# A routed expert layer behind linear attention: the fullest expert's left rows join its own job, and rows are asked for one job further ahead

## The chip, the cores and the metric

The kernel runs on one core of one Trainium2 chip. The time is the device time of one launch in microseconds (us), the median of a few runs. A separate, profiled execution gives the trace that is read below; its own time stands beside its span, the stretch from the first instruction to the last.

A core has five engines that run their own instruction streams and meet at semaphores: PE (matrix products), DVE and ACT (element-wise work on 128 partitions), POOL (element-wise work, and DMAs whose addresses come from an index list) and SP (here a queue that issues DMAs). In the profile "PEld" is PE's weight load.

## What is computed

Linear attention, normalised, followed by a layer of eight experts in which each row goes to one expert. Cut to what matters:

```python
# q, k, v: (8, 8, 576, 64)
kv  = einsum('bhsd,bhse->bhde', k, v)
out = einsum('bhsd,bhde->bhse', q, kv)
out = out / sqrt(mean(out * out, -1) + 1e-6) * g_norm
x = out.transpose(0, 2, 1, 3).reshape(4608, 512)

logits = x @ w_gate                      # 4608 x 8
expert = argmax(logits, 1)
gate   = softmax(logits)[row, expert]
for e in range(8):                       # w1[e]: 512 x 1024, w2[e]: 1024 x 512
    rows = expert == e
    y[rows] = gate[rows] * (relu(x[rows] @ w1[e]) @ w2[e])
```

How many rows an expert gets depends on the data. The inputs are drawn with a fixed seed.

## The kernel before

**Attention, 36 slots.** The 4608 rows are taken in 36 slots of 128 rows, nine to a pair of batches. k, v and q of one batch are each one load of 1.18 MB through SP (`load`, L201, issued at L207) into ten landing buffers `land`. For each batch PE forms k-transposed times v (`kv_mm`, L235, 64x64 tiles, L244). For each slot POOL brings q into order (`x_qp`, L297, instruction L302), PE transposes it (`x_qt`, L308, L312), ACT copies it, PE multiplies it with kv (`x_mm`, L326, L335). ACT and DVE normalise. The order of the slots and of all work inside them is written out by hand (`plan`, the lists `mid`, `late`, `last`, L810 to L894): POOL orders q three slots ahead, the transposition runs two slots ahead, and the kv products of a batch are spread over the four slots from the sixth before its first slot.

**Routing.** `Route` (L388) finds each row's expert and its rank among that expert's rows, and POOL scatters each row (1032 bytes: 512 half-precision values, the row's number, the sum for its gate) to place `expert * 4608 + rank` of a table `xs` in HBM (`scatter`, L480, L483). Places that get no row must not hold stray numbers. `blank_rows` (L221) therefore writes, early in the attention stage, 128 empty rows ahead of row 608 of each expert from a constant `c_zero` (L222), and the marks of the 32 rows that follow (L228). Both DMAs stand in SP's queue between the loads of k and v of batch 3 and that of q of batch 3 (L930 to L932).

**Expert jobs.** The experts are worked off one after the other, each as one job (`Job`, L634) of at most 608 rows (`CAP`), whatever the data: `CT` = 5 blocks of 128, 128, 128, 128 and 96 rows. The expert with the most rows among the last four (`FIXED` = 4) changes places with expert 7 and comes last; which it is, a chain of small DVE operations finds once all rows are counted (`left_over_table`, L526). SP reads the expert's number from it into a register (`expert_at`, L776).

A job consists of:
- `fetch` (L644): a transposing DMA of the job's rows from `xs` into `xt` (L654), and a small DMA of the rows' numbers and sums, `mt` (L662). `xt` has three buffers.
- `one` (L707): the first product. For each of two column ranges of 304 rows and eight blocks of the hidden size, four matmuls (L698) into `hp` (four buffers) and a relu on ACT (L710) into `ht`, a part of `xh`.
- `two` (L738): the second product. For each block of rows, eight matmuls of 512 columns (L743) into `yp` (four buffers), a DVE multiplication with the gate into `ys` (L748), and a scatter of the rows to the output on POOL (L751).
- `place` (L674): three small DVE operations that turn `mt` into indices and gates.

The weights of each expert are two loads of 2 MB (L159 for w1, L165 for w2) through SP into five staging buffers, taken in a fixed order by `load_next` (L191). While job n runs its products, DVE casts w1 of job n+1 (L171) and ACT casts its w2 (L182).

Job 0 is woven into the end of the attention stage (L985 to L1038). The order of the rest is the loop at L1044: at its head `jobs[n + 2].fetch()`, then the first product, a weight load, the second product, for n = 0 the table, then `place` of the next job and another weight load. So in SP's queue the rows of job n+2 stand behind the weight loads that job n-1 issued.

**The left rows.** Rows of the last expert beyond 608 form a job of their own, `left_over(32, ...)` (L782), of up to 128 rows. It runs seventh, just ahead of the last expert, with that expert's weights: POOL gathers the rows (L625), PE transposes them (L770) inside job 6, and both products follow on their own. Should rows still be left, a loop on a register (L1085) takes them 128 at a time.

Of the kernel before, what the change touches and what calls it, by code (L numbers as in the profile page):

```python
# [28 lines left out]
def kernel(  # L29
# [20 lines left out]
    CAP = 608  # L50
    EARLY = 384
    NE = EARLY // 128
    NOV = (N - CAP) // 128 + 1
    WIDTHS = [128, 128, 128, 128, 96]
# [14 lines left out]
    c32 = np.zeros((128, 128 + 8 + 8 + CT + 36 + 1 + 32), np.float32)  # L69
# [15 lines left out]
    c32[:, o_t:o_t + 32] = np.arange(32)  # L85
    c_f32 = nc.inline_tensor(c32, name="c_f32")
# [10 lines left out]
    zr = np.zeros((32, 4, RW // 2), np.float32)  # L97
    zr[:, :, RW // 2 - 1] = 1.0
    c_zero = nc.inline_tensor(zr.reshape(32, 2 * RW).view(np.int32), name="c_zero")
# [15 lines left out]
    tcol = cf[:, o_t:o_t + 32]  # L115
    ident16 = ch[:, 0:128]
# [10 lines left out]
    nvf = fixed("nvf", [128, 33], F32)  # L127
# [3 lines left out]
    tabb = fixed("tabb", [128, 33], F32)  # L131
    tabi = fixed("tabi", [128, 2, 40], I32)
    blank = fixed("blank", [128, RW // 2], I32)
    xo_bufs = [fixed(f"xo{n}", [128, RW], F16) for n in range(2)]
# [10 lines left out]
    xh = [fixed(f"xh{n}", [128, 8 * CAP], F16) for n in range(2)]  # L145
# [3 lines left out]
    order = list(range(E - 1)) + ["left", E - 1]  # L149
# [36 lines left out]
    W = [Weights(e, n) for n, e in enumerate(range(E))]  # L186
    W.append(W[E - 1])
# [33 lines left out]
    def blank_rows():  # L221
        nc.sync.dma_start(  # L222
            xs.ap().rearrange("(e s) c -> e s c", e=E)[:, CAP - 128:CAP, :].rearrange(
                "e (p r) c -> e p (r c)", r=4
            ),
            _bc(c_zero.ap(), 0, E),
        )
        nc.sync.dma_start(  # L228
            xs.ap().rearrange("(e s) c -> s e c", e=E)[CAP:CAP + 32, :, 256:258],
            _bc(blank[0:32, 256:258], 1, E),  # L230
        )
# [294 lines left out]
    def left_over_table():  # L526
# [16 lines left out]
        def pick(out, what):  # L543
# [28 lines left out]
        )  # L572
        nc.vector.tensor_scalar(
            nvf[:, 32:33], most_n, -float(CAP), None, op0=ALU.add
        )
        nc.vector.tensor_scalar(
            tabb[:, 32:33], who, float(N), float(CAP), op0=ALU.mult, op1=ALU.add
        )
        nxt = PW.tile([128, 8], F32, tag="nxt")
        nc.vector.tensor_scalar(nxt, most, 128.0, float(CAP), op0=ALU.mult, op1=ALU.add)  # L580
# [16 lines left out]
        cmb = PW.tile([128, 32, 8], F32, tag="cmb")  # L597
# [12 lines left out]
        nc.vector.reduce_sum(nvf[:, 0:32], cm, axis=AXX)  # L610
        nc.vector.scalar_tensor_tensor(
            out=nvf[:, 0:32], in0=tk, scalar=-128.0, in1=nvf[:, 0:32], op0=ALU.mult, op1=ALU.add
        )
        nc.vector.tensor_scalar(tabi[:, 0, 8:40], te, 7.0, None, op0=ALU.min)
        sb = tabb[:, 0:32]
# [18 lines left out]
    class Job:  # L634


        def __init__(self, nt, w, n, row, okm, bgm, views):
            self.nt, self.w, self.row = nt, w, row
            self.n = n
            self.okm, self.bgm, self.views = okm, bgm, views  # L640
            self.cols = CAP if nt > 1 else 128
            self.spans = [(0, 304), (304, CAP)] if nt > 1 else [(0, 128)]

        def fetch(self, t0=0, t1=None):  # L644
            nt = self.nt
            t1 = nt if t1 is None else t1
            if t0 == 0:
                self.xt = PW.tile([128, 4, CAP], F16, tag="xt", bufs=3, name="xt")
                self.mt = PW.tile([128, nt, 2], I32, tag=f"mt{nt}", bufs=4, name="mt")
            c0, c1 = 128 * t0, min(128 * t1, CAP)  # L650
# [17 lines left out]

            for go in (marks, rows) if self.n > 1 else (rows, marks):
                did = go()  # L670
                if t1 == NE:
                    early_reads.append(did)

        def place(self, t0=0, t1=None, okm=None, bgm=None):  # L674
# [11 lines left out]
            )  # L686
            nc.vector.tensor_tensor(self.idx[:, t0:t1], self.raw[:, t0:t1], bgm, op=ALU.add)
# [50 lines left out]
        def two(self, t, yp=None):  # L738
            m = WIDTHS[t]
            if yp is None:  # L740
                yp = PSF.tile([128, D], F32, tag="yp", bufs=4, name="yp")
            for f in range(8):
# [3 lines left out]
                )  # L746
            ys = PW.tile([128, D], F32, tag="ys", bufs=5, name="ys")
# [380 lines left out]
```

## Time and profile before

| | |
|---|---|
| median of 3 runs | 271.66 us (271.3 to 273.56) |
| profiled execution | 271.03 us, span 269.1 us |
| PE busy | 242.2 us (90%), 2708 matmuls |
| ACT busy | 155.2 us (58%) |
| DVE busy | 143.9 us (53%) |
| POOL busy | 107.5 us (40%) |
| granted clock of PE | 0.999 |
| moved by DMA | 82.93 MB, mean 308 GB/s |
| weight loads, 2 MB each | 16, median 12.6 us from issue to landing |
| transposing loads of rows | 9, median 9.7 us from issue to landing |

How to read it: a line of the timeline gives start (us), length (us), engine, line of the kernel, operation, what is written and what is read, and how many instructions were merged; in brackets the idle time of the engine before it and what ended it. "SPq" is a DMA issue in SP's queue: its length is the time that SP is held by it, not the transfer. "Landing" is the time from the start of an issue to the semaphore that tells of its end.

The page's rows of slices, 6.7 us each (busy tenths of PE and of DMA):

```profile
PE   5996799899999987689699999999899999999992
DMA  7999999999999999496799999999999999942023
```

The attention stage fills slices 1 to 20, the expert jobs those behind them.

### The profile page before, as it was taken

The numbers are of one execution on the slowest core, as the hardware profiler recorded it, in microseconds if no ns is written. First come the engines' busy times: TensorE is split into PE (matmuls) and PEld (weight loads), VectorE is DVE, ScalarE is ACT, GpSimd is POOL, SyncE is SP. The second block draws the span as 40 slices with busy tenths as digits, with TensorE's granted clock in tenths as the row PEclk, the third lists the DMA queues.
The fourth block names the chain that finished last, engine by engine and source line by source line (L and its number), as shares of the span: only waits on it lengthen the run. The fifth ranks groups of instructions, "written<-read, shape, count | busy, mean of one in ns | idle before, by whom it ended". The sixth has DMA issues, their size and how long they took to land. (4 is left out here: it accounts for less than half of the span.)

```text
span 269.1 us, 6877 instructions
## 1 busy us (share of the span) xinstructions
PE 242.2 (90%) x2708; PEld 170.4 (63%) x2708; DVE 143.9 (53%) x374; ACT 155.2 (58%) x359; POOL 107.5 (40%) x138
## 2 busy tenths in 40 slices
PE   5996799899999987689699999999899999999992
PEld 1575688788878876554457466574564756747740
DVE  1004277688787769988728991453604525343031
ACT  1053668567677748688248648287284692754800
POOL 8032222387378286557511060522404415042142
PEclk9999999999999999999999999999999999999999
DMA  7999999999999999496799999999999999942023
GB/s 241 333 391 391 392 426 369 394 397 392 393 382 407 415 384 355 161 274 256 168 221 410 250 328 417 277 384 332 362 420 277 375 314 322 285 125 104 14 79 110
DMA packets 52002, 82.93 MB, mean 308 GB/s; under 512 B 27739, under 2 KB 27995, under 8 KB 51944
## 3 DMA queue, kind: packets, MB, share of 16 engines
q1 hardware_dynamic: 46464, 67.95, 75.9%
q0 software_dynamic: 5056, 14.26, 14.3%
q8 instruction: 22, 0.36, 0.6%
q10 hardware_dynamic: 448, 0.26, 0.5%
q14 instruction: 12, 0.10, 0.1%
HBM read 63.37 MB, written 16.04 MB: 295 GB/s over the span
## 5 line engine op out<-in xcount | busy, mean ns | idle before, releaser
L751 POOL DMA_INDIRECT out_dram<-ys,idx x41 | 41.2, 1005 | 95.3 <-DVE ys L748 86.1
L710 ACT ACTIVATE xh<-hp 128x304 f16<-128x304 f32 (+1 forms) x120 | 49.2, 413 | 46.3 <-PE hp L698 33.2
L743 PE MATMUL yp<-w2b,xh 128*128 128x512 f16 (+1 forms) x304 | 67.1, 379 | 0.6 <-ACT xh L734 0.6
L698 PEld LDWEIGHTS <-w1b 128*128 128x128 f16 x544 | 51.7, 98 | 22.6 <-issue 5.5
L748 DVE TENSOR_SCALAR ys<-yp,gate 128x512 f32<-128x512 f32 (+1 forms) x38 | 28.2, 749 | 69.2 <-PE yp L743 69.2
L698 PE MATMUL hp<-xt,w1b 128*128 128x304 f16 (+1 forms) x480 | 61.1, 288 | 1.2 <-DMA xt<-xs_scratch 1.2
L743 PEld LDWEIGHTS <-xh 128*128 128x128 f16 (+1 forms) x328 | 33.6, 103 | 36.2 <-issue 0.8
L483 POOL DMA_INDIRECT xs_scratch<-xh,sli x36 | 36.2, 1006 | 29.4 <-DVE xh L475 10.2
L335 PE MATMUL op<-kvs,qts 128*128 128x144 f32 (+1 forms) x320 | 44.2, 295 | 1.4 <-issue 1.4
L335 PEld LDWEIGHTS op<-kvs,qts 128*128 128x128 f32 (+1 forms) x320 | 37.1, 179 | 4.6 <-issue 1.9
L357 DVE TENSOR_REDUCE ms<-sq 128x8 f32<-128x512 f32 x36 | 24.6, 684 | 23.5 <-ACT sq L353 23.0
L353 ACT ACTIVATE sq<-op 128x512 f32<-128x512 f32 x36 | 21.4, 594 | 18.5 <-PE op L335 12.6
L244 PE MATMUL kvp<-land 64*64 64x64 f32 x1152 | 24.7, 229 | 7.0 <-issue 3.8
L302 POOL COPY qp<-land 128x512 f32<-128x512 f32 x32 | 19.6, 616 | 25.8 <-DMA land<-in_q_dram 15.0
L244 PEld LDWEIGHTS kvp<-land 64*64 64x64 f32 x1152 | 20.7, 140 | 13.1 <-issue 12.9
L182 ACT CAST w2b<-land 128x1024 f16<-128x1024 f32 x28 | 27.2, 1043 | 0.0
L373 DVE TENSOR_TENSOR xh<-op,rinv 128x512 f16<-128x512 f32 x36 | 24.5, 680 | 0.3 <-PE op L457 0.3
L312 PE MATMUL qtp<-cf,qp 128*128 128x128 f32 x144 | 22.1, 276 | 1.5 <-POOL qp L302 1.5
L318 ACT COPY qts<-qtp 128x512 f32<-128x512 f32 x36 | 20.9, 581 | 1.3 <-PE qtp L312 1.2
L171 DVE TENSOR_SCALAR w1b<-land,g 128x1024 f16<-128x1024 f32 x28 | 19.5, 751 | 0.0
L312 PEld LDWEIGHTS qtp<-cf,qp 128*128 128x128 f32 x144 | 16.6, 141 | 3.0 <-POOL qp L302 1.9
L255 ACT COPY kvs<-kvp 64x256 f32<-64x256 f32 x16 | 5.8, 360 | 16.2 <-PE kvp L244 16.1
(128 smaller groups left out, 166.7 us busy)
## 6 DMA issues: line engine op xcount, KB each, us to landing
land<-in_moe_w_dram SPq DMA_DIRECT2D x16, 2048.0 KB, 12.6
land<-in_q_dram SPq DMA_DIRECT2D x8, 1152.0 KB, 16.8
land<-in_k_dram SPq DMA_DIRECT2D x7, 1152.0 KB, 16.9
land<-in_v_dram SPq DMA_DIRECT2D x7, 1152.0 KB, 16.1
land<-in_k_dram SPq DMA_DIRECT2D x2, 576.0 KB, 4.2
land<-in_v_dram SPq DMA_DIRECT2D x2, 576.0 KB, 7.4
xs_scratch<-c_zero SPq DMA_DIRECT2D x1, 1032.0 KB
out_dram<-ys,idx POOLq DMA_INDIRECT x41, 6.3
```

What stands on the lines that cost most here:

```text
L182: nc.scalar.copy(self.w2[:, part, :], self.s2[:, part, :])
L244: nc.tensor.matmul(kvst[b][HALF[ipar], hh, Dh * ip:Dh * ip + Dh], kb[HALF[hh], i, cols], vb[HALF[hh], i, cols], start=(j == 0), stop=(j == 8),
L312: nc.tensor.transpose(qtps[s][:, ip, :, tok, :], qps[s][:, tok, 2 * ip:2 * ip + 2, :], ident)
L335: nc.tensor.matmul(ops[s][cols, i4, 0:144], qts[s][:, i4, cols], kvs[:, i4, :], start=True, stop=True,)
L357: nc.vector.reduce_sum(ms, sq, axis=AXX)
L373: nc.vector.tensor_tensor(xg[:, r, 0:512].rearrange("p (i c n) -> p c i n", i=2, c=4), oc[:, :, 0:128].rearrange("p c (i n) -> p c i n", i=2),
L483: go = nc.gpsimd.indirect_dma_start(out=xs_views[9 * self.P + g0 + t], out_offset=IndirectOffsetOnAxis(ap=self.sli[:, t:t + 1], axis=0), i ...
L698: nc.tensor.matmul(hp, self.w.w1[:, 2 * (kk % 2) + kk // 2, f // 2 * 256:f // 2 * 256 + 256] .rearrange("p (m r) -> p r m", r=2)[:, f % 2, :],
L710: nc.scalar.activation(self.ht[:, f, c0:c1], hp, ACTF.Relu)
L743: nc.tensor.matmul(yp[0:m, :], self.ht[:, f, t * 128:t * 128 + m], self.w.w2[:, f, :], start=(f == 0), stop=(f == 7),)
L748: nc.vector.tensor_scalar(ys[0:m, :], yp[0:m, :], self.gate[0:m, t:t + 1], None, op0=ALU.mult)
L751: nc.gpsimd.indirect_dma_start(out=self.views[t], out_offset=IndirectOffsetOnAxis(ap=self.idx[0:m, t:t + 1], axis=0), in_=ys[0:m, :], in_o ...
```

## The change

- The last expert's job takes up to `LAST` = 672 rows. Its first product runs over two ranges of 336 columns. Its second product has six blocks: five of 128 rows and one of 32. For the block of 32, `two` issues 32 matmuls of 128 columns: each 128-column quarter of the output goes to its own group of 32 PE columns and 32 output partitions, so that the result stands as 128 partitions of 128 values. It is scattered as quarter rows, with indices four times the row's number plus the quarter.
- The job for left rows goes, with its place in the order, its gather, transposes, second row buffer and index operations. The loop for further left rows stays, from row 672 of the last expert on.
- `left_over_table` makes masks for the last job (`lvalid`, `lbigm`) instead of the two entries of the left job.
- Rows are fetched one job further ahead: job 2's ahead of the two weight loads at the end of the attention stage, and `jobs[n + 3]`'s behind the first product of job n, ahead of the weight loads of that turn. The last job's fetch has four more small DMAs, which bring the marks of its last 32 rows to four groups of 32 partitions.
- `blank_rows` writes the empty rows in two DMAs: rows 480 to 608 of experts 0 to 3, and rows 480 to 672 of experts 4 to 7. The constant has 48 rows, each with two values of padding. Marks of rows 608 to 640 are written for experts 0 to 3 alone.
- The drain of POOL behind job 6 moves to job 5; one work tile shares the space of another.

```diff
     CAP = 608
+    LAST = 672
...
-    zr = np.zeros((32, 4, RW // 2), np.float32)
-    zr[:, :, RW // 2 - 1] = 1.0
-    c_zero = nc.inline_tensor(zr.reshape(32, 2 * RW).view(np.int32), name="c_zero")
+    zr = np.zeros((48, 4 * (RW // 2) + 2), np.float32)
+    zr[:, RW // 2 - 1:2 * RW:RW // 2] = 1.0
+    c_zero = nc.inline_tensor(zr.view(np.int32), name="c_zero")
...
-    xh = [fixed(f"xh{n}", [128, 8 * CAP], F16) for n in range(2)]
+    xh = [fixed(f"xh{n}", [128, 8 * (CAP, LAST)[n]], F16) for n in range(2)]
...
     def blank_rows():
+        by_e = xs.ap().rearrange("(e s) c -> e s c", e=E)
+        for e0, e1, end in ((0, FIXED, CAP), (FIXED, E, LAST)):
+            n = (end - CAP + 128) // 4
+            nc.sync.dma_start(
+                by_e[e0:e1, CAP - 128:end, :].rearrange("e (p r) c -> e p (r c)", r=4),
+                _bc(c_zero.ap()[0:n, 0:2 * RW], 0, e1 - e0),
+            )
         nc.sync.dma_start(
-            xs.ap().rearrange("(e s) c -> e s c", e=E)[:, CAP - 128:CAP, :].rearrange(
-                "e (p r) c -> e p (r c)", r=4
-            ),
-            _bc(c_zero.ap(), 0, E),
-        )
-        nc.sync.dma_start(
-            xs.ap().rearrange("(e s) c -> s e c", e=E)[CAP:CAP + 32, :, 256:258],
-            _bc(blank[0:32, 256:258], 1, E),
+            by_e.rearrange("e s c -> s e c")[CAP:CAP + 32, 0:FIXED, 256:258],
+            _bc(blank[0:32, 256:258], 1, FIXED),
         )
...
-        nc.vector.tensor_scalar(
-            nvf[:, 32:33], most_n, -float(CAP), None, op0=ALU.add
-        )
+        nc.vector.tensor_scalar(lvalid[:, 0:CT], rankc, most_n, None, op0=ALU.is_lt)
         nc.vector.tensor_scalar(
-            tabb[:, 32:33], who, float(N), float(CAP), op0=ALU.mult, op1=ALU.add
-        )
+            lvalid[:, CT:CT + 1], in_q, 128.0 * CT, most_n, op0=ALU.add, op1=ALU.is_lt
+        )
+        nc.vector.tensor_scalar(lbigm, lvalid, -BIG, BIG, op0=ALU.mult, op1=ALU.add)
+        nc.vector.tensor_tensor(
+            lbigm[:, CT:CT + 1], lbigm[:, CT:CT + 1], of_q, op=ALU.add
+        )
...
+            self.cols = {1: 128, CT: CAP, CT + 1: LAST}[nt]
+            mid = self.cols // 2 if nt > 1 else 0
+            self.spans = [(0, mid), (mid, self.cols)] if mid else [(0, 128)]
...
+            if nt > CT:
+                for m in range(4):
+                    nc.sync.dma_start(
+                        self.mt[32 * m:32 * m + 32, CT, :],
+                        xs.ap().rearrange("(e s) c -> e s c", e=E)[
+                            mine, 128 * CT:LAST, 256:258
+                        ].rearrange("o s c -> (o s) c"),
+                    )
...
+            if t == CT:
+                for f in range(8):
+                    for c in range(4):
+                        nc.tensor.matmul(
+                            yp[32 * c:32 * c + 32, 0:128], self.ht[:, f, 128 * CT:LAST],
+                            self.w.w2[:, f, 128 * c:128 * c + 128],
+                            start=(f == 0), stop=(f == 7),
+                        )
+                self.put(t, 128, 128, yp, self.views[t].rearrange("n (q c) -> (n q) c", q=4))
+                return
...
         jobs[1].fetch()
+        jobs[2].fetch()
         load_next(2)
...
-        for n in range(len(order)):
+        for n in range(E):
             job = jobs[n]
-            if n == 3:
-                jobs[7] = left_over(32, W[7], 7, 0, out_views[E * CT])
...
-            if n + 2 < len(order) - 1:
-                jobs[n + 2].fetch()
-            if n == 5:
-                jobs[8].fetch()
...
+            if n + 3 < E:
+                jobs[n + 3].fetch()
             if nxt is not None:
                 load_next()
             for t in range(NE if n == 0 else 0, job.nt):
                 job.two(t)
...
-            if n in (2, 6):
+            if n in (2, 5):
                 nc.gpsimd.drain()
```

`put` is the former end of `two` (the copy L748 and the scatter L751) with the number of partitions and columns as arguments.

## The prediction

> **What bounds it now.** I read the page first: PE is busy in 242.2 us of the 269.1 us span, at full clock, and DMA shows 9 tenths or more in almost every slice up to the thirty-fifth. The chain of waits is of no use here: it ends after 1 us (a scatter and its queue). So I went to the timeline of each engine, stage by stage. In the expert stage (from 140 us) PE runs without gaps but one:
>
> ```profile
> 192.30 8.43 PE L698 MATMUL hp<-xt,w1b 128*128 128x304 f16 x64 [1.21 <-DMA xt<-xs_scratch]
> ...
> 243.22 1.95 PE L698 MATMUL hp<-xt,w1b 128*128 128x128 f16 x32
> ...
> 245.00 1.89 PE L743 MATMUL yp<-w2b,xh 128*128 128x512 f16 x8
> ...
> 246.73 8.43 PE L698 MATMUL hp<-xt,w1b 128*128 128x304 f16 x64
> ...
> 255.00 8.80 PE L743 MATMUL yp<-w2b,xh 128*128 128x512 f16 x40
> ...
> 264.86 0.92 POOL L751 DMA_INDIRECT out_dram<-ys,idx  x1 [0.74 <-DVEq L1084]
> ```
>
> To see: job 4 waits for its rows; the left job holds PE from 243.22 to 246.73; behind the last matmul come a DVE copy and a scatter. The timeline of SP's queue says why rows are late:
>
> ```profile
> 171.66 0.38 SPq L159 DMA_DIRECT2D land<-in_moe_w_dram  x1
> 172.26 0.45 SPq L662 DMA_DIRECT2D mt<-xs_scratch  x1
> 172.90 14.65 SPq L654 DMA_TRANSPOSE xt<-xs_scratch  x1
> 187.79 0.39 SPq L165 DMA_DIRECT2D land<-in_moe_w_dram  x1
> ```
>
> The transposing load holds SP until the weights ahead of it have landed (issued 171.66, landing 15.7 us later, at 187.4; SP is free at 187.55). Rows and weights share one queue that is never empty: what is asked for first comes first. The attention stage, which the change seems not to touch, has the same queue, and the zero rows go through it:
>
> ```profile
> 27.16 1.64 SPq L222 DMA_DIRECT2D xs_scratch<-c_zero  x1
> 28.91 1.11 SPq L228 DMA_DIRECT2D xs_scratch<-blank  x1
> 30.06 1.37 SPq L207 DMA_DIRECT2D land<-in_q_dram  x1
> ```
>
> The busy times by stretch (PE, PEld, DVE, ACT, POOL, clock, DMA share, GB/s) show DMA full before, during and after it:
>
> ```profile
> 26.00:36.00 10.00, 7.42 (x119) 6.74 (x119) 3.30 (x8) 5.81 (x17) 2.58 (x6) 1.00 1.05 390
> 36.00:42.00 6.00, 5.99 (x136) 5.11 (x133) 4.54 (x12) 4.42 (x12) 1.69 (x3) 1.00 1.05 411
> 42.00:52.00 10.00, 9.19 (x212) 8.14 (x213) 7.05 (x20) 6.19 (x18) 2.83 (x4) 1.00 1.04 389
> ```
>
> **What the Trainium skill says.** "DMA: Bandwidth & Descriptors", section "Why a DMA increments its semaphore by 16 and not by 1": a DMA is spread over the largest k up to 16 that divides the slowest dimension (over 1) of both access patterns, on SP's queue the lowest-numbered k engines. The trace agrees for 8: c_zero is written with the 8 experts outermost, and its packet records are 24 packets of 44,032 bytes, 1.63 us each, in eight back-to-back runs of three (36.4 to 42.7 us); meanwhile the rate of the q, k, v packets falls from about 170 to 85 per us, half. The same page, "Queues, rings and completion order": each engine takes its ring in order. No run yet shows 4 engines. "TensorEngine Tiling (Array Packing)", "Tiling Modes": column tiles run in parallel; the 64x64 matmuls of L244 agree (40 in 0.81 us, 20 ns apart, though one takes some 218 ns).
>
> **The change, part by part.** Counting the reference's choices on these inputs gives 564, 494, 600, 572, 539, 654, 585, 600 rows, so expert 5 is last in both kernels: 46 left rows before, none over 672 after; the loop for the rest (L1085) stays off in both.
>
> 1. *Left job gone.* PE 243.22 to 246.73: -3.51. Its four transposes inside job 6 (L770): the first product there takes 226.09 to 234.59, 8.50, against 209.19 to 217.46, 8.27: -0.23. Its gather, three index operations and copy lie beside PE work: 0. The drain on POOL moves from job 6 to job 5: POOL idles 8 to 10 us before each job's first scatter, so 0; the memset of the second row buffer goes while POOL waits 7.24 us for q: 0.
>
> 2. *336 columns for 304 in the last job.* 64 matmuls of 304 take 246.73 to 255.00, 129.2 ns each; of 128 columns 243.22 to 245.00, 55.6 ns. That is 0.418 ns a column: 142.6 ns, times 64: +0.86. The fifth block with 128 rows for 96 costs PE nothing: 379 ns in both forms.
>
> 3. *The last 32 rows.* 32 matmuls of 128 columns: 8 x 55.6 = 0.45 us side by side, 32 x 55.6 = 1.78 in turn; not less than 0. Then a 128x128 copy, which I put at 0.35 from the 0.75 of 512 columns. But POOL bounds it: after block four ends on PE (X), its copy (0.75), 0.28 to POOL, scatter 0.98, gap 0.30, last scatter 0.95 end at X+3.3; in turn they end at X+3.6. Before, the end is X+0.03+0.75+0.28+0.92 = X+2.0. So +1.3 to +1.6; I take +1.4, landing unchanged.
>
> 4. *The table* (L526). Two 128x1 operations go (0.06 us apart), four come: two free (0.10, 0.06) and two that wait for the one before (0.20 each, as L582 and L583 stand): +0.44 on DVE. Behind it on DVE are the four w1 casts and the first ys of job 1, ending 155.27; PE's fifth block (148.43 + 4 x 1.73 = 155.35) needs the yp that this frees. Cover 0.08, so +0.36 (between 0, if PE's start has more play than the records show, and 0.44).
>
> 5. *Rows one pair ahead.* Job 2's rows now precede both weight loads of 135.11 and 136.02; each weight load falls behind by one fetch, some 3.7 us (135.1 to 138.8: SP must wait for job 1's rows and marks, which land at about 138). The wait at job 4 goes: job starts are 16.90, 16.97, 18.27, 16.89, 16.90 apart, so -1.3. Who is late next: w2 of job 6, landing 216.2 before, 219.9 after, cast by ACT while PE does the second product from 216; four casts of about 0.97 end at 223.8, and the next relu is due at about 225.3. Cover 1.5 us, and four hp buffers more (2.1). The four added mark DMAs of the last job (some 0.5 each on SP) stand under the 16 us landing of the weights ahead: 0; without that cover +2.
>
> Parts 1 to 5: -3.51 -0.23 +0.86 +1.4 +0.36 -1.3 = **-2.4**.
>
> 6. *Zero rows* (L221). The one DMA with 8 experts outermost becomes two with 4 outermost, and a padded source, so rows no longer merge: 4 x 32 and 4 x 48 pieces of 4128 bytes. By the skill's rule k is 4 for both, on the same engines. A 4096-byte packet takes 159 ns in this trace, so each of the four gets 80 x 160 ns = 12.8 us of work instead of 3 x 1.63 = 4.9: **7.9 us** more, in order, ahead of q of batch 3 and everything behind it. Each later load needs those engines too, and DMA stays full up to about 102 us, so the lateness is not worked off. What it meets:
>
> ```profile
> 47.14 0.63 POOL L302 COPY qp<-land 128x512 f32<-128x512 f32 x1
> ...
> 52.39 0.60 PE L312 MATMUL qtp<-cf,qp 128*128 128x128 f32 x4
> ...
> 56.42 0.81 PE L244 MATMUL kvp<-land 64*64 64x64 f32 x40
> ```
>
> q of batch 3 (issued 30.06, landing 16.8 later) comes at 54.8 for 46.9; POOL's copy ends 55.4, and PE wanted it at 52.39: 3.1 lost. v of batch 4 lies between landings at 49.8 and 60.0, about 52.9; at 60.8 it is 4.4 late for PE's 56.42. v of batch 5 (46.21 + 17.4 = 63.6) comes at 71.5 for PE's 66.73: 4.8. Later loads have 5 to 7 us of slack. At the end w2 of job 1 lands at 119.8 for 111.9, and job 0's rows (issued 112.9, used 117.8, 1.0 of slack) queue behind it: up to 1.1 more. So 4.8 to 5.9, I take **+5.5**. On no more than six engines or so the work exceeds 8.0 us and begins to show; on sixteen it would be 3.2 us, and nothing.
>
> Sum: -2.4 + 5.5 = +3.1 on the span, 272.2; the profiled execution lasted 271.03 with a span of 269.1, so 274.1. That execution is 0.6 below the median of the three runs; on 271.66 the same gives **274.8 us**.
>
> **Rivals.** *Zeros spread* (ends on the other side): the padded pieces go over eight or more engines, 128 and 192 of them being divisible by 16. Then only -2.4 counts: 269.3, or 268.6 if other work covers the table and the final landing, of a third of the bytes, is 0.3 shorter. For it: packets of 44 KB no longer block an engine for 1.63 us; against it: eight outermost gave eight engines. *Slow zeros*: pieces that start off a boundary, HBM to HBM, take 200 ns rather than 160: 3.2 us more, 278.0; nothing of this form stands in the trace. *Slack absorbs it*: loads further on wait for buffers (PE and POOL held SP 4 to 6 us several times), so a late stretch is partly worked off: 2.5 us of slip, 271.8. *Weights late*: the 3.7 us eat the cover of part 5; each us beyond it adds one; I give it inside the ranges.
>
> **Numbers.** As forecast 0.58 (273.3 to 276.5, of which 0.38 slower by over 1% and 0.20 within); spread 0.24 (half and half faster and within); slow zeros 0.11; absorbed 0.07. A change of 1% is about what can be told from none here. That gives faster 0.12, within 0.39, slower 0.49. The range 268.6 to 277.0 leaves out the lower half of the spread case and the slow zeros, less than 2 in 10 with what strays.
>
> **What will show it.** Zero packets of 4128 bytes in four runs; q, k, v landings some 8 us later from q of batch 3; PE or POOL idle for it near 52 to 60; then no wait at job 4, 336-column matmuls near 143 ns, and the last scatter 3.3 us behind block four. If the landings near 47 to 64 us stand where they stood, part 6 is wrong and the kernel is faster.

## The result, and the profile after

| | median (runs) | range | profiled execution | its span |
|---|---|---|---|---|
| before | 271.48 us (4) | 271.23 to 273.56 | 271.03 us | 269.1 us |
| after | 279.75 us (4) | 277.66 to 280.73 | 279.46 us | 277.3 us |

The ratio is 1.0285, with a 95% interval of 1.0216 to 1.0355: slower by some 8 us. The forecast was 274.8, range 268.6 to 277.0. Executions of one kernel differ by up to 4%, and every ratio and interval below counts only those within 1.5% of that kernel's fastest.

I read the profile of after in the order in which its time goes. First SP's queue in the timeline (start, duration, instruction), where before had 1.64 and 1.11 us for the zero rows and their marks:

```profile
27.01 5.22 SPq L229 DMA_DIRECT2D xs_scratch<-c_zero  x2
32.34 4.91 SPq L233 DMA_DIRECT2D xs_scratch<-blank  x1
37.30 0.43 SPq L211 DMA_DIRECT2D land<-in_q_dram  x1
37.83 7.67 SPq L211 DMA_DIRECT2D land<-in_k_dram  x1
...
56.49 2.72 SPq L211 DMA_DIRECT2D land<-in_v_dram  x1
```

q of batch 3 is issued at 37.30 for 30.06, the k load behind it holds SP for 7.67 us, and v of batch 5 is issued at 56.49 for 46.21: the queue is 7 us late at once and 10 us late a little further on. The busy times by stretch (the columns are those of before) say what the DMA engines do meanwhile:

```profile
36.00:42.00 6.00, 6.00 (x137) 5.19 (x137) 4.55 (x12) 4.42 (x12) 1.74 (x3) 1.00 0.94 321
42.00:52.00 10.00, 9.30 (x215) 8.15 (x215) 8.02 (x23) 7.32 (x22) 0.08 (x1) 1.00 0.70 215
52.00:62.00 10.00, 4.66 (x38) 4.49 (x39) 2.06 (x6) 2.09 (x7) 5.87 (x8) 0.66 1.02 377
```

From 42 to 52 they moved 215 GB/s for 389 before, at a share of 0.70 for 1.04, and POOL did next to nothing (0.08 us). The packet records say why: 320 packets of 4128 bytes, 160 ns each in the median and 172 in the mean, run from 37.4 to 52.5 us, mostly at 21 to 26 per us, so that about four are under way at any moment; of the 128 eight-byte packets of the marks, which come behind them, 96 ran at 37 to 39 us and the last 32 at 51 to 52. That is twelve engines that were free and four that were not. From 43 to 46 us no data of q, k or v moved. The rule in the Trainium skill that I had used ("DMA: Bandwidth & Descriptors", section "Why a DMA increments its semaphore by 16 and not by 1") thus holds for four as it did for eight.

POOL stood still for a reason of its own, which the prediction does not have. In its timeline before and after, the copy of q stands behind the first scatter of rows into `xs`:

```profile
46.09 1.06 POOL L483 DMA_INDIRECT xs_scratch<-xh,sli  x1 [3.95 <-DVE xh L475]
```

```profile
54.07 1.05 POOL L488 DMA_INDIRECT xs_scratch<-xh,sli  x1 [11.98 <-DVE cum L442]
56.68 0.61 POOL L307 COPY qp<-land 128x512 f32<-128x512 f32 x1 [1.56 <-DMA land<-in_q_dram]
```

That scatter writes to the table that the zero rows go to. It starts 1.5 us after the last zero packet has ended in after (52.5), in after_order (53.04 for 51.5) and in k4 (53.24 for 51.7), two runs that come further down, and after_order's profile names the DMA of the marks as what ended the wait. So the bracket's "cum" is a semaphore that merely came last. With q on time the copy would still have had to wait until 55.12; the late q added 1.56 us. No run separates these two ways from the zero rows to PE.

What PE meets, in its timeline (the bracket is the idle time ahead and what ended it):

```profile
57.34 1.11 PE L317 MATMUL qtp<-cf,qp 128*128 128x128 f32 x4 [6.05 <-POOL qp L307]
...
59.11 1.95 PE L340 MATMUL op<-kvs,qts 128*128 128x144 f32 x8
...
63.25 0.81 PE L249 MATMUL kvp<-land 64*64 64x64 f32 x40 [0.97 <-DMA land<-in_v_dram]
...
74.65 0.81 PE L249 MATMUL kvp<-land 64*64 64x64 f32 x40 [0.58 <-DMA land<-in_v_dram]
...
127.76 1.53 PE L725 MATMUL hpe<-xt,w1b 128*128 128x384 f16 x8 [2.31 <-DMA xt<-xs_scratch]
...
142.59 4.89 PE L725 MATMUL hpl<-xt,w1b 128*128 128x224 f16 x32 [2.40 <-DMA xt<-xs_scratch]
```

For job 0's late rows and the start of job 1, before had:

```profile
132.85 3.23 PE L698 MATMUL hpl<-xt,w1b 128*128 128x224 f16 x32 [2.33 <-DMA xt<-xs_scratch]
...
140.16 8.43 PE L698 MATMUL hp<-xt,w1b 128*128 128x304 f16 x64
```

The matmuls that stood at 52.39, 56.42 and 66.73 stand at 57.34, 63.25 and 74.65. Then the slip of the attention slots stays at 7.9 us to the end (slot 35 starts at 124.25 for 116.35), job 0's early rows (hpe) add 1.8, and job 0's late rows (hpl) take 4.89 us for 3.23 although they are the same matmuls. The 59.11 line shows the same thing: 1.95 us for 1.25. The granted TensorE clock stood at one half from 53.9 to 60.8, 129.0 to 132.4 and 142.7 to 146.1 us; before it stood at full from 12.8 us to the end. Each begins inside an idle time of PE or within 1.3 us behind it: the 6.05, the 2.31 and the 2.40 us of the lines above. Such an idle time does not always bring one: before idles 2.33 us ahead of hpl at full clock.

Last the expert stage, PE's timeline and then POOL's last line:

```profile
151.56 8.43 PE L725 MATMUL hp<-xt,w1b 128*128 128x304 f16 x64
...
167.25 1.89 PE L780 MATMUL yp<-w2b,xh 128*96 128x512 f16 x8 [0.35 <-DVE ys L788]
168.97 8.43 PE L725 MATMUL hp<-xt,w1b 128*128 128x304 f16 x64
...
202.77 8.43 PE L725 MATMUL hp<-xt,w1b 128*128 128x304 f16 x64
...
253.47 9.28 PE L725 MATMUL hp<-xt,w1b 128*128 128x336 f16 x64
262.59 8.80 PE L780 MATMUL yp<-w2b,xh 128*128 128x512 f16 x40
271.32 0.63 PE L772 MATMUL yp<-w2b,xh 128*32 128x128 f16 x32
```

```profile
273.74 0.98 POOL L791 DMA_INDIRECT out_dram<-ys,idx  x1 [0.30 <-issue]
```

There is no left job, no wait for rows at job 4 (202.77), and the table costs the 0.35 us in the bracket of 167.25. From job 1's start to the last expert's start it is 101.91 us for 106.57; from there to POOL's end 21.25 for 19.05. So the stage that the change is about became shorter, as forecast, and job 1 starts 11.40 us later (151.56 for 140.16), where +5.5 was forecast.

### The profile page after: what moved, and what is told of

It reads as the page before. It is cut to its first block, busy times and chain, and to the rows that moved or that the text cites. A ratio compares the mean times of both kernels' runs of the same rounds, so it can differ in the third digit from the quotient of the medians.

```text
span 277.3 us, 6845 instructions
## 1 busy us (share of the span) xinstructions
PE 243.7 (88%) x2696; PEld 170.9 (62%) x2696; DVE 141.4 (51%) x370; ACT 154.4 (56%) x351; POOL 105.3 (38%) x135
## 4 chain that ended last, share of the span: by engine, by line
issue 29%; DMA 27%; PE 19%; POOL 12%; SPq 4%; ACT 3%; DVE 2%; POOLq 1%; ACTq 0%
DMA land<-in_v_dram 14%; POOL out_dram L791 9%; DMA out_dram<-ys,idx 8%; PE op L340 7%; PE kvp L249 5%; SPq L211 4%; DMA xt<-xs_scratch 3%; DMA xs_scratch<-xh,sli 3%; PE qtp L317 3%; POOL xs_scratch L488 2%; PE hpl L725 2%; PE yp L780 1%; ACT sq L358 1%; PE kgp L280 1%; POOLq L1113 1%
## 5 line engine op out<-in xcount | busy, mean ns | idle before, releaser
L737 ACT ACTIVATE xh<-hp 128x304 f16<-128x304 f32 (+1 forms) x112 | 47.8, 428 | 43.0 <-PE hp L725 29.9
L780 PE MATMUL yp<-w2b,xh 128*128 128x512 f16 (+1 forms) x296 | 65.4, 379 | 1.0 <-ACT xh L761 0.6
L788 DVE TENSOR_SCALAR ys<-yp,gate 128x512 f32<-128x512 f32 (+2 forms) x38 | 27.7, 738 | 70.1 <-PE yp L780 70.1
L725 PE MATMUL hp<-xt,w1b 128*128 128x304 f16 (+1 forms) x448 | 59.9, 294 | 0.0
L780 PEld LDWEIGHTS <-xh 128*128 128x128 f16 (+1 forms) x320 | 32.6, 102 | 36.3 <-issue 1.4
L340 PE MATMUL op<-kvs,qts 128*128 128x144 f32 (+1 forms) x320 | 45.0, 299 | 1.4 <-issue 1.4
L340 PEld LDWEIGHTS op<-kvs,qts 128*128 128x128 f32 (+1 forms) x320 | 38.0, 182 | 4.5 <-issue 1.8
L358 ACT ACTIVATE sq<-op 128x512 f32<-128x512 f32 x36 | 21.4, 594 | 19.5 <-PE op L340 12.8
L176 DVE TENSOR_SCALAR w1b<-land,g 128x1024 f16<-128x1024 f32 x28 | 19.4, 747 | 0.0
L370 DVE TENSOR_TENSOR lr<-op,rinv 128x64 f32<-128x64 f32 x36 | 7.9, 221 | 17.8 <-ACT rinv L368 17.4
```

Source lines behind the costliest of these rows:

```text
L340: nc.tensor.matmul(ops[s][cols, i4, 0:144], qts[s][:, i4, cols], kvs[:, i4, :], start=True, stop=True,)
L725: nc.tensor.matmul(hp, self.w.w1[:, 2 * (kk % 2) + kk // 2, f // 2 * 256:f // 2 * 256 + 256] .rearrange("p (m r) -> p r m", r=2)[:, f % 2, :],
L737: nc.scalar.activation(self.ht[:, f, c0:c1], hp, ACTF.Relu)
L780: nc.tensor.matmul(yp[0:m, :], self.ht[:, f, t * 128:t * 128 + m], self.w.w2[:, f, :], start=(f == 0), stop=(f == 7),)
L788: nc.vector.tensor_scalar(ys[0:m, 0:d], yp[0:m, 0:d], self.gate[0:m, t:t + 1], None, op0=ALU.mult)
```

## The experiments

My theory after this: the zero rows on four engines are the loss, larger than I had made it because of the lateness of the queue and of the clock. The rivals: the loss comes from the rows that go ahead of the weights, or from the clock alone. The kernels ran in four sessions on three chips; the medians of before were 273.49, 273.49, 271.62 and 270.95 us there, so every ratio is to before in the same session. Between two sessions, ratios that differ by less than 1% say little: the change and one other kernel ran in two, and their ratios differ by 0.4%, their plain medians, set against those of before, by up to 0.8%.

**Zero rows over sixteen engines, nothing else (z16).**

```diff
-  by_e[e0:e1, CAP - 128:end, :].rearrange("e (p r) c -> e p (r c)", r=4),
-  _bc(c_zero.ap()[0:n, 0:2 * RW], 0, e1 - e0),
+  by_e[e0:e1, CAP - 128:end, :].rearrange("e (p r) c -> p e (r c)", r=4),
+  _bc(c_zero.ap()[0:n, 0:2 * RW], 1, e1 - e0),
```

> The changed kernel with one edit: the empty rows are written with the piece number outermost (32 and 48) instead of the expert, the same bytes in the same pieces. Theory (four engines carry all zero pieces): sixteen engines now get 20 pieces each, 3.2 us of work for 4.9 in the kernel before; q of batch 3 lands by 47 us, PE does not wait for it, its clock stays full, and the attention stage keeps the pace of the kernel before. The expert stage keeps its gain of some 2.5 us and the shorter landing 0.7: span about 266, time about 268, ratio 0.987. Rival (0.26 MB more, 320 small pieces in place of 24 large ones, or rows asked for earlier slow the attention stage): it stays above 276.

Measured: 1.0025 (0.9991 to 1.006). The attention stage recovered: PE waited for neither q of batch 3 nor v of batches 4 and 5. But the time is that of before and not 1.3% below it, as expected, so the zero rows are not all of it. The timeline of PE in the expert stage shows a wait that after does not have:

```profile
158.99 1.89 PE L780 MATMUL yp<-w2b,xh 128*96 128x512 f16 x8 [0.35 <-DVE ys L788]
160.71 3.78 PE L725 MATMUL hp<-xt,w1b 128*128 128x304 f16 x28
164.65 5.47 PE L725 MATMUL hp<-xt,w1b 128*128 128x304 f16 x36 [0.16 <-ACT xh L737]
```

Job 2's first product took 9.25 us (160.71 to 169.96) for 8.27: PE waited for ACT's relus. Why they were late is open: ACT had cast w2 of job 2 by 156.0, and its timeline has no other work between the relus.

**The zero rows alone, put into the kernel before (before_z4).** The diff is the new `blank_rows` and the padded `c_zero` of the change, with 672 for LAST.

> The kernel before with the changed writing of empty rows alone (two DMAs with four experts outermost, padded source). Theory: the whole loss of the attention stage appears here: q of batch 3 lands near 56 us, PE waits some 6 us for it, the clock drops; 279 to 283 us. Rival (the loss needs the other parts of the change): 271 to 273.

Measured: 1.02 (1.0117 to 1.0283). PE's timeline has the two waits of after:

```profile
57.09 0.73 PE L313 MATMUL qtp<-cf,qp 128*128 128x128 f32 x4 [2.51 <-POOL qp L303]
...
63.33 0.81 PE L245 MATMUL kvp<-land 64*64 64x64 f32 x40 [1.32 <-issue]
```

The waits are shorter, since a half clock from 26.8 to 37.1 us had made PE late by then, but the matmuls stand where they stand in after (57.34 and 63.25), and job 1 starts at 147.96 for 140.16. Most of the loss appears with this edit alone, in a kernel that has the left job and the old order of rows.

**Eight engines (z8).** One DMA with the eight experts outermost, which writes the marks of all experts too, so that their own DMA goes:

```diff
-  for e0, e1, end in ((0, FIXED, CAP), (FIXED, E, LAST)):
+  for e0, e1, end in ((0, E, LAST),):
```

> The changed kernel with one zero DMA of rows 480 to 672 of all eight experts, expert outermost, and no separate marks for experts 0 to 3. Theory, with the point of 3.1 us of slack: eight engines get 48 pieces each, 7.7 us, 2.8 more than before: just hidden; 268 to 269 us. Rival (bytes or pieces count, not engines; this writes 0.3 MB more than the changed kernel): 280 or more.

Measured: 1.0039 (0.9996 to 1.0082). The same as before, and 0.14% above z16; 268 to 269 us had been expected, as for z16. It writes 384 pieces where the change writes 320, so the number of pieces is not what costs.

**Products of zeros where PE stood idle (warm, warm2).** warm adds 26 products of 128x512 at slot 11 and 10 behind slot 35; warm2 the same 26, and the 10 ahead of hpl:

```diff
+  at(mid, 11, zeros, 26)
...
+  zeros(10, "op", 2)
   for n, tag in enumerate(("kvp", "op", "op", "misc")):
       job.late_pair(2 * n, tag)
```

> The changed kernel with matmuls on zeros put into PE's stream where it idles: 26 of 512 columns between slot 11's product and the transposition of slot 13 (5.7 us), 10 behind slot 35's product (2.2 us). Theory (part of the loss is PE's clock, halved after an idle stretch): the granted clock stays full, the first products after the wait take 1.25 us for 1.95, and 2 to 4 us come back: 276 to 278. Rival (the clock costs nothing, since DMA sets the pace there): 279 to 280.

> The change as it is (zero rows on four engines), with products of zeros wherever PE stood idle: 26 of them at slot 11, where PE waits for q of batch 3, and ten ahead of hpl. Theory (11.4 us of lateness at job 1's start are 5.5 us of queue, some 2.4 us of half clock in the attention stage, 1.6 us of half clock at hpl, and 1.8 us of rows and clock ahead of job 0's first product): with the clock kept up job 1 starts at about 147.5 to 148.5 instead of 151.56, hpl takes 3.2 us, and the span is 273.5 to 274.5, time 275.5 to 276.5, some 3.5 us below the change. Rival (the clock is a companion, not a cause: the queue alone sets when job 1 starts, and what is won in the attention stage is waited for at job 0's rows): job 1 starts within 1 us of 149.7 and the median is within 1 us of the change's 279.5.

Measured: 1.0188 (1.0114 to 1.0263) and 1.0167 (1.0082 to 1.0252). In warm no half clock fell between 32 and 141 us and slot 35 started at 121.83, 2.4 us earlier than in after and 5.5 later than before. Not all of that is the clock: PE still waited for v of batch 5 (0.70 us, at 72.90 for 74.65), so the load itself came earlier, and slot 35 differs by over 1 us between profiles without such products (124.25 in after, 123.69 in k4, 124.95 in after_order). Job 1 started at 149.73, 1.8 us earlier than in after. In warm2 none fell from 38 us to the end of the last expert's matmuls and hpl took 3.23 us, yet job 1 started at 149.92 and the span was 277.5: a half clock of 10.2 us early in the attention stage and a wait of 0.85 us had put slot 11's product at 54.92 us for 50.05, the 26 products ended after q had come, and job 2 waited 0.75 us for ACT. Both ratios are 0.6 to 1.2% below the two of the change (1.0285, and 1.0248 further down), with intervals that overlap. The clock's share in the median stays open; it is at most some 3 us.

**The order of rows and weights, with sixteen engines (z16_order, z16_hpl, z16_tuned).** z16_order takes the rows back to the head of a job:

```diff
-  jobs[2].fetch()
   load_next(2)
...
+  if n + 2 < E:
+      jobs[n + 2].fetch()
...
-  if n + 3 < E:
-      jobs[n + 3].fetch()
```

> The z16 kernel (the change with its zero rows over sixteen engines), but with the rows asked for in the old order: job n+2's at the head of job n, behind both weights of job n+2. Theory A (part 5 of the prediction is worth 1.3 us and the new 0.7 to 1.0 us wait of job 2's first product on ACT is its price): the wait of job 4 for its rows of about 1.2 us is back, the wait on ACT in job 2 is gone, so against z16's median the time is +0.2 to +0.6 us, and against before it stays about 1.5 us below what before takes, were it not for the clock. Rival B (rows ahead are what spoils z16): job 2's wait is gone, no wait at job 4 returns, and the time is 1 us or more below z16. Rival C (the clock decides, not the order): no difference from z16 beyond the half-clock stretches, which I count.

Measured: 0.9887 (0.9839 to 0.9934), 1.4% below z16 with intervals that don't touch. Rival B is right: the rows ahead are what spoils z16. How they do it the profiles of the two do not show: 1.4% is 3.8 us, the slow relus in job 2 account for 1.0 in one execution of z16, and z16_order waits 0.28 us for ACT there as well. The wait at job 4 didn't return in z16_order's profile (job 4 started 17.18 us after job 3 for 16.90), but with the same order it did in others: 1.80 us in best_b, and 2.05 at job 3 in k16, both below.

z16_hpl is z16 with the ten products ahead of hpl.

> The z16 kernel with ten 128x512 products of zeros on PE between job 0's first three output blocks and its late rows (hpl), where PE stands idle 2.4 us for rows. Theory (that idle time is what brings a half-clock stretch of 3.4 us onto hpl): hpl takes 3.2 us instead of 4.8, job 1 starts 1.5 us earlier against job 0's first output block, and the median is 1 to 1.6 us below z16, 272.5 to 273.3 on this chip where before has some 273.9. Rival (the half clock comes whatever PE does there, or moves to another place): hpl still about 4.8 us, or the same 1.6 us lost elsewhere, and the median within 0.5 us of z16.

Measured: 0.9963 (0.9913 to 1.0012). Its interval overlaps that of z16, so no gain is shown.

z16_tuned adds to z16_hpl the masks lvalid and lbigm taken behind job 1's output blocks, and asks for job 2's rows where before does and for job 3's one pair ahead, behind the w2 of job 3:

> z16_hpl with two more edits: job 2's rows asked for behind its two weights, as before, and rows ahead of the weights only from job 3 on (job 3's between the w1 and w2 of its own pair); and the four operations on lvalid and lbigm taken out of the table and put behind job 1's output blocks. Theory: the 0.35 us wait for ys in job 1 goes, the wait on ACT in job 2 goes (0.7 to 1.0 us), no wait at job 4; against z16_hpl -1.0 to -1.4 us, so 271 to 272 where before has 273.9: the first version that is faster than before by about 1%. Rival: the late w2 only moves from job 2 to job 3 and the same 0.7 to 1.0 us is lost there; then -0.35 us against z16_hpl.

Measured: 1.0093 (1.0054 to 1.0132), a miss: I had made it slower. PE's timeline, and then ACT's, of this kernel:

```profile
197.35 6.36 PE L730 MATMUL hp<-xt,w1b 128*128 128x304 f16 x48 [1.94 <-ACT xh L742]
...
232.68 6.36 PE L730 MATMUL hp<-xt,w1b 128*128 128x304 f16 x48 [1.33 <-ACT xh L742]
```

```profile
193.10 3.89 ACT L187 CAST w2b<-land 128x1024 f16<-128x1024 f32 x4 [7.79 <-DMA land<-in_moe_w_dram]
```

To see: ACT waits for w2 to land (7.79 us), casts it for 3.89 us, and only then gets to the relus for which PE waits. My edit had put two sets of rows between the w2 of job 3 and that of job 4, and the lead lost there did not come back. The number that goes with these times is how long before its job a w2 is asked for, read from SP's queue and PE's timeline. For job 4: 21.3 us in before (171.02, 192.30), 21.0 in z16_order, 21.7 in k16, 19.4 in z16 (176.10, 195.49), 19.8 in after (183.01, 202.77), 10.1 in z16_tuned (183.07, 193.18). Some 1.6 to 2.3 us of lead are what the rows take by going ahead of the weights; that PE waits for w2 when so little is gone is not shown, for in the profiles of z16 and after ACT waits for a w2 by 1.07 us at most, and PE not at all behind it.

**Controls (after_order, best_a, best_b, before_z16).** after_order is the change with the edit of z16_order; before_z16 is before_z4 with the edit of z16; best_a is z16_order with the late masks; best_b adds the ten products ahead of hpl.

> The change (zero rows on four engines), but with the rows asked for in the old order, behind the weights. Theory A (PE comes to job 1 some 11 us later than before, so the queue has a lead and job 4's rows are there in either order: part 5 buys the change nothing): no wait for rows at job 4, the wait of job 4 does not return, and the time is within 0.5 us of the change's 279.5. Rival B (part 5 is worth its 1.3 us): the wait at job 4 is back at about 1.2 us and the time is 1.3 us above the change. Rival C (rows ahead cost the change what they cost z16, where taking them back brought 1.4%): 2 us or more below the change.

> z16_order (zero rows over sixteen engines, rows behind weights as before) with the four operations on lvalid and lbigm put behind job 1's output blocks. Theory: the 0.36 us wait for ys in job 1 is gone, nothing else moves: 0.3 to 0.4 us below z16_order, ratio to before about 0.987, so 271 where before has 274.5. Rival (w2 of the next job bounds there, the wait only moves into job 2's first product on ACT): no difference.

> best_a with ten products of zeros ahead of hpl. Theory (a half-clock stretch falls on hpl in some executions, costing 1.6 us): hpl at 3.2 us in every profile and the median 0 to 1 us below best_a. Rival (the ten products, 2.3 us, end after the rows have come and themselves hold hpl, or the clock falls elsewhere): the median 0 to 0.5 us above best_a.

> The kernel before with only the padded zero rows, over sixteen engines. Theory (5 us or less of work for each engine is hidden; before's zeros on eight engines cost nothing): the same as before within 0.5%, so the 1.1% that z16_order has over before come from the left job and its neighbours. Rival (the spread zeros themselves make the attention stage faster): 0.7% or more below before, with job 1 starting earlier than 140.2.

Measured: after_order 1.0177 (1.0122 to 1.0233); best_a 0.9914 (0.9889 to 0.994); best_b 0.9946 (0.9909 to 0.9982); before_z16 1.0053 (1.0023 to 1.0082). Spread zeros bring before nothing (0.5% slower, if anything), so what best_a wins comes from its other parts. Late masks bring nothing that can be seen: best_a was expected at 0.987 and is no faster than z16_order (0.9887), though the wait of 0.35 us for ys is gone in k16, which is the same kernel. after_order is 0.7 to 1.1% below the two ratios of the change, nearest its rival C, with intervals that overlap. The ten products bring no gain either: hpl took 3.23 us with them, and 4.89 in the profile of z8 without, but also 3.23 in that of k16 without.

**One kernel with three widths of the zero rows, and the change beside it (k4, k8, k16, change).** k16 is best_a; k8 and k4 are best_a with the zero DMA of z8 (one DMA, which writes the marks of all experts too) and of the change; all four ran on one chip.

> best_a's kernel with the zero rows of the change: four engines, 80 pieces of 4128 bytes each, 12.8 to 15 us of work for each. Theory (the work of the busiest engine beyond some 8 us is lateness of every load behind it, of which 3.1 us is slack, and the clock adds 1 to 2): 6.5 to 8.5 us above k16, 275.5 to 277.5 where k16 has 269. Rival (the loss of the change was mostly part 5 and the clock): 4 us or less above k16.

> The same with the zero rows in one DMA over eight engines, 48 pieces each, 7.7 us at 160 ns. Theory: 7.7 for 4.9 us of before is 2.8 us later at most, within the 3.1 us of slack at v of batch 5: 0 to 0.7 us above k16. Rival (there is no threshold, each us of work on the busiest engine costs its share): half of k4's loss, 3 us or more above k16.

> best_a's kernel again, on the same chip as k4 and k8: 16 to 20 pieces an engine, 3.2 us or less. It is the zero point of the three: 0.986 to 0.995 of before.

> The change as it is, on the same chip as k4. Theory A (with zeros on four engines PE comes late to the expert stage and the weights are there in either order): 0 to 0.7 us above k4, of which 0.36 is the masks. Theory B (rows ahead cost the change what they cost z16): 2.5 to 4 us above k4, with PE waiting on ACT's relu behind late w2 casts in some executions.

| zero rows on | rows behind the weights | rows ahead of the weights |
|---|---|---|
| 4 engines | k4 1.0197 (1.016 to 1.0233), after_order 1.0177 | the change 1.0285 (1.0216 to 1.0355) and 1.0248 (1.0161 to 1.0335) |
| 8 engines | k8 0.998 (0.9953 to 1.0008) | z8 1.0039 (0.9996 to 1.0082) |
| 16 engines | k16 0.9876 (0.979 to 0.9962), best_a 0.9914 (0.9889 to 0.994) | z16 1.0025 (0.9991 to 1.006) |

PE's timeline of k4 (the wait for q of batch 3, then the starts of jobs 1, 3 and 7), and that of k16 (the same starts, no wait for q):

```profile
56.51 1.12 PE L317 MATMUL qtp<-cf,qp 128*128 128x128 f32 x4 [5.68 <-POOL qp L307]
...
150.96 8.43 PE L730 MATMUL hp<-xt,w1b 128*128 128x304 f16 x64
...
184.76 8.43 PE L730 MATMUL hp<-xt,w1b 128*128 128x304 f16 x64
...
252.36 9.28 PE L730 MATMUL hp<-xt,w1b 128*128 128x336 f16 x64
```

```profile
141.77 8.43 PE L730 MATMUL hp<-xt,w1b 128*128 128x304 f16 x64
...
177.78 8.43 PE L730 MATMUL hp<-xt,w1b 128*128 128x304 f16 x64 [2.05 <-DMA xt<-xs_scratch]
...
245.37 9.28 PE L730 MATMUL hp<-xt,w1b 128*128 128x336 f16 x64
```

In the program only the number of engines differs: job 1 is 9.2 us later in k4 and the last expert 7.0, since k16 waits for rows (2.05) where k4, being late, doesn't. In ratios, four engines cost 2.8 to 3.2% over sixteen (1.0197 against 0.9914 and 0.9876), 7.7 to 8.7 us, as the theory said (6.5 to 8.5), and eight cost 0.7 to 1.0%, 1.8 to 2.8 us, where 0 to 0.7 was expected. The sizes are less sure than these intervals look: k16 counts four executions, the change three, and the plain medians of what is counted are 275.66 us for k4, 271.43 for k8, 270.47 for k16, 279.68 for the change and 270.95 for before. By these four engines cost 5.2 us over sixteen and eight 1.0. So the order is shown; the size is some 5 to 9 us for four engines and 1 to 3 for eight. In k8 the first product of job 0 waits for rows:

```profile
121.57 1.46 PE L726 MATMUL hpe<-xt,w1b 128*128 128x384 f16 x8 [2.56 <-DMA xt<-xs_scratch]
```

Of these 2.5 us (119.03 in k16) 1.0 is left at hpl, and z8's profile has no such wait, so where the loss with eight engines falls is open. Down the table the loss grows with the work on the busiest engine. Across it, rows ahead are dearer in each row: by 0.5 to 1.1% with four engines, 0.6% with eight, 1.1 to 1.5% with sixteen. Only in the last row are the intervals apart; for the change itself that it pays for its rows is likely and not shown. k4, k8, k16 and best_a also have late masks (0.35 us, 0.13%), which the kernels on the right have not; z16 against z16_order is free of that.

## Why the prediction was wrong

The direction and the main mechanism were right; the size was off by 5 us. On the profiled span 272.2 was forecast and 277.3 measured, 8.2 us over before: +11.4 up to job 1's start, -4.7 from there to the last expert, +2.2 from there to POOL's end, -0.7 in the landing.

- **Parts 1 to 3, the left job, 336 columns, the last 32 rows: right.** From job 1's start to the last expert's start the profile shows -4.66, for -4.68 with parts 4 and 5 (-3.51 -0.23 +0.36 -1.3). The last expert's first product takes 9.12 us, as worked out; from its start to POOL's end +2.2, for +2.26. The matmuls on four groups of 32 columns ran side by side (0.63 us for 32), and the last scatter of POOL starts 1.28 behind the one ahead. The landing is 0.7 us shorter, which I had given to a rival. Free of the zero rows and of part 5 this is a gain: k16 and best_a, which have only these parts, are 0.9 to 1.2% below before, 2.3 to 3.4 us, for some 2.2 by my sum (-1.48, and -0.7 of landing); by plain medians best_a is 2.7 and k16 only 0.5 us below.
- **Part 4, the table: right.** +0.35 in the bracket, for +0.36.
- **Part 5, rows ahead: right in this profile, wrong as a gain.** The wait at job 4 went, though by luck. But the sentence "Cover 1.5 us" was the step to doubt: the lead of w2 fell by 2 us. The rows ahead cost z16 1.4%, and how is open: that a w2 asked for too late makes PE wait on ACT is shown for z16_tuned alone, where some 11 us of lead were gone. The pairs of runs show +0.5 to +1.5% instead of -1.3 us, with intervals apart only on sixteen engines. The rival *Weights late* had that mechanism; I had given it no chance of its own. I had also counted the wait at job 4 as if PE came there on time; with PE 11 us late the rows are there in the old order too (after_order waits 0.15 us at job 3 and nowhere later).
- **Part 6, the zero rows: the step that failed, in its size.** "80 x 160 ns = 12.8 us of work instead of 3 x 1.63 = 4.9: 7.9 us more" set engine time against engine time. With four, the pieces took 172 ns each in the mean, 13.8 us of work for each engine, and the first of them began a us later than before, so that the zeros ended at 52.5 for 42.7: 9.8 us later in place of 7.9. q of batch 3 landed as much later, at 56.7 for 46.9 (54.8 forecast), and v of batch 5 at 74.6 for 63.6 (71.5 forecast). So v came 11.0 us later: 7.9 us too late for PE in place of 4.8. What lies between 9.8 and 11.0 fits a loss that I had not counted, the idle time of the other twelve engines: SP feeds all sixteen, and the issues behind the zero rows took it 4.91 and 7.67 us, in which the twelve ran dry (215 GB/s). No run tries that part by itself. Nor does the prediction have POOL's scatter waiting for the zero rows; it cost nothing beyond the late q here, but a q that is loaded ahead of the zero rows would still have met it.
- **Job 0's rows: up to +1.1 forecast, +1.8 measured**, with a wait of 2.31 us and a half clock from 129.0 to 132.4 on them.
- **The clock: not in the sum.** The Trainium skill ("TensorE: Matmul & The Clock Gate", section "Part 1: The HAM clock gate (the "warmup" mystery)") says that the clock is halved after an idle window of about 3.4 us and that the windows run freely; the stretches here last 3.41 us or twice that, as it says, but two of the three follow idle times of 2.31 and 2.40 us, shorter than the page's window. The one on hpl cost 1.66 us. That makes 7.9 + 1.8 + 1.7 = 11.4 in this profile. Whether the clock costs as much in the median is open: z16_hpl and best_b, which keep PE busy ahead of hpl, show no gain over z16 and best_a.

Of the rivals, *Zeros spread* falls (four engines at a time), *Slow zeros* holds for a third (172 ns in the mean, not 200: 1.0 of its 3.2 us), and that its time, 278.0, was nearest is luck, and *Slack absorbs it* falls: the queue fell further behind.

A version that beats both kernels came out of it: zero rows over sixteen engines and rows behind the weights, 0.9887 of before (z16_order), and with masks late 0.9914 and 0.9876 (best_a, k16).

## What to carry to other kernels

For a DMA in a full queue look at how its outermost dimensions divide, and cost it by the time until its busiest engine is done, plus what the other engines lose while the issuing queue is held; here the order of two dimensions in the pattern was worth 2 to 3% of the kernel. Look also for what else must wait until that DMA has landed, as POOL's scatter did here. Before loads are reordered in a full queue, read for each load how long before its use it is asked for, and leave that lead where it is shortest. A wait that one execution shows and an upstream delay would hide is not a gain that can be added to a sum with that delay in it.

## What the hardware showed that I had not expected

- The issue of DMAs on SP is itself slow behind a DMA on few engines: 5.22 us for the two zero DMAs, 4.91 for 1 KB of marks, 7.67 for a k load that took 2.81 before. With the zero rows over sixteen engines the two took 3.54 and the marks 1.39.
- Stretches of half clock come in 3.41 us or two or three times that (while PE works; the one at the very end is cut off), and at different places from execution to execution of one kernel: before had none after 12.8 us in its profile; z16 and before_z16, which do not wait for the zero rows, had three and two of 3.41 us in theirs.
- A transposing load of an expert's rows held SP for 9.9 to 15.7 us in the expert stage of k16. That this is what makes a set of rows ahead of a w2 so dear fits z16_tuned, and was not tried by itself.
